# Room for a sixth raw weight pair, and the snapshots' pool opened behind the weight conversion

## The chip, the cores and the metric

The kernel runs on one core of one Trainium2 chip. The metric is the device time of one launch in microseconds (us), as the median of several runs. Before the change it is 868.43 us (three runs, 868.04 to 869.34).

The engines are named as in the profile: PE is the matrix engine and PEld its weight loads, DVE the vector engine, ACT the scalar engine, POOL the GpSimd engine, SP the engine that here issues nearly all DMAs. Each engine works through its own instructions in the order in which the program lists them; they meet at semaphores.

## The reference

Two blocks follow each other. An attention without softmax gives, by batch and head, a 64 x 64 matrix of keys by values, multiplies the queries with it and normalises each row; its output is reshaped to 4608 tokens of 512 features, and a feed-forward block with a squared ReLU follows.

```python
kv = np.einsum('bhsd,bhse->bhde', k, v)            # batch 8, heads 8, seq 576, dim 64
out = np.einsum('bhsd,bhde->bhse', q, kv)
rms = np.sqrt(np.mean(out * out, axis=-1, keepdims=True) + 1e-06)
x = (out / rms * g_norm)                           # -> (4608, 512)
h = x @ w_in                                       # (512, 2048)
r = np.maximum(h, 0.0)
return (r * r) @ w_out                             # (2048, 512)
```

The two weights arrive as 64-bit floats. The kernel reads them as 64-bit words and builds 32-bit floats from them.

## The kernel before

The 4608 tokens are cut into nine strips of 512. A strip is first multiplied "up" with `w_in`, then "down" with `w_out`; both products are made with Strassen-like schemes (seven products of half-size blocks in place of eight, in the later strips two levels deep), so sums and differences of weight blocks and of activations are needed beside the products. The order of the work is written out by hand: for each strip a list of steps, and between them the attention's slices for the next strips.

**Strip 0 is the opening, and the change lies in it.** Its 16 up steps (`up_first`, line 911, from 33.6 to 82.4 us in the profile) are plain products. Between them the weights are converted, one pair of pieces at a time (`convert`, with the table `PACE` that says how many conversions are done behind each step). One pair of pieces goes through these stages:

- SP asks for its two halves of 512 KB (`load_piece`, line 248) into a place of `raw_pool`; there are five places, each 8 KB per partition.
- ACT makes two passes over it (`act_words`, lines 260 and 262), into one of two `w_c` buffers and back into the raw place.
- POOL clamps (line 282), DVE puts the bits together in two passes (lines 284 and 288) into the 32-bit weight.
- For the last four of the sixteen pairs (`sums_out`) the result goes into a tile `wt`, which also has its room in `raw_pool`; DVE makes four sums there (line 306), and SP stores `wt` to DRAM as parts of `w_out`, four DMAs of 256 KB for each `wt` (line 336). Two further blocks go out at line 344.

`load_more` runs behind each conversion and asks for pieces up to `AHEAD` pieces beyond the converted ones: ten pieces are five pairs, as many as there are places. SP's queue is one list: the loads of keys, values and queries of the next batch (lines 135, 150, 165, 173), the raw pairs and the stores stand in it in the order in which the program issues them, and a DMA also waits for the semaphore that the eighth DMA before it used.

When the sixteen up steps are done, the rest is converted and the conversion's pools are closed (`conv.close()`, line 1402). In their room two pools open: `stream` (six tiles of 8 KB, weights streamed from DRAM) and `sum` (eight tiles of 2 KB). Both are opened with `reuse_waits="tile"`.

**The snapshots' pool** `c_pool` has six tiles of 2 KB per partition and is opened at line 92 with the long-lived pools, so it has room of its own. It holds copies of PSUM banks ("snapshots", `combine`, line 880), output tiles (`out_tile`, line 977) and, from strip 1 on, squares of attention outputs (line 493, through `query`). Its first tile is the snapshot of product 1 of strip 0's down pass.

**The work around that first snapshot**, in program order. Strip 0's down pass (`down`, line 870) runs its products in the order 1, 2, 5, 6, 7, 3, 4. ACT's list there reads: copy of transposed queries (line 422), the snapshot (line 880), two copies of the key-value matrices of batch 1's last pair of heads into `kv_all` (lines 453 and 454), squares of attention outputs (line 493). PE's list: product 1 (line 870), keys by values of that last pair (line 448), the attention outputs `x_ps` of two token tiles (line 484, pair of heads by pair of heads, the last pair last), product 2. The fourth pair of heads in line 484 needs the copies of lines 453 and 454. SP's list: the stores of the third and fourth `wt` (line 336), then the first streamed weights (line 965).

Of the kernel before, what the change touches and what calls it, by code (L numbers as in the profile page):

```python
# [20 lines left out]
def kernel(  # L21
# [56 lines left out]
    BEHIND = 1.6  # L78
    X_ON_PE = 2
    EPS = 1e-6  # L80
    AHEAD = 10
    PACE = (3, 4, 4, 5, 6, 7, 8, 9, 10, 11, 12, 13, 13, 14, 15, 16)
    const = ctx.enter_context(tc.tile_pool(name="const", bufs=1))
    wpool = ctx.enter_context(tc.tile_pool(name="wpool", bufs=1))
# [4 lines left out]
    small = ctx.enter_context(tc.tile_pool(name="small", bufs=3))  # L89
    g_pool = ctx.enter_context(tc.tile_pool(name="g", bufs=4))  # L90
    dram = ctx.enter_context(tc.tile_pool(name="dram", bufs=1, space=bass.MemoryType.DRAM))
    c_pool = ctx.enter_context(tc.tile_pool(name="c", bufs=6))
    conv = ExitStack()
    xt_pool = conv.enter_context(tc.tile_pool(name="xt", bufs=1))
    raw_pool = conv.enter_context(tc.tile_pool(name="raw", bufs=5))
    spare_pool = conv.enter_context(tc.tile_pool(name="spare", bufs=1))
    wtmp = conv.enter_context(tc.tile_pool(name="wtmp", bufs=2))
    psums = ExitStack()
# [62 lines left out]
    def load_rest(b, eng):  # L161
        h = b % 2 * (b > Q_ON_PE + 1)
        half = slice(REST * h, REST * (h + 1))
        for t, src in ((k_rest[half], k), (v_rest[half], v)):
            eng.dma_start(out=t, in_=src[b, :, C * P : S].rearrange("h s d -> s h d"))
# [20 lines left out]
    def load_next(q_eng=nc.sync, names="kvq"):  # L186
        u = next(to_load, None)
        if u is not None:
            load(*u, q_eng, names)
# [49 lines left out]
    raw = []  # L239
    raw_pairs = []  # L240

    def load_piece():
        i = len(raw)
        if i < len(sources):
            if i % 2 == 0:
                raw_pairs.append(raw_pool.tile([P, 2, 2, WN // 2], I64, name="raw", tag="raw"))
            t = raw_pairs[i // 2][:, i % 2]
            nc.sync.dma_start(out=t, in_=sources[i])
            raw.append(t)
# [50 lines left out]
    def load_more(end):  # L300

        while len(raw) < min(end + AHEAD, max(len(sources) - 4, end + AHEAD - 4), len(sources)):
            load_piece()
# [38 lines left out]
    def store_first(b):  # L342
        for e in range(2):
            nc.sync.dma_start(out=w_out[b, :, e], in_=w_first[b][:, :, ts(e, P)])
# [427 lines left out]
    def attend(n):  # L772
        while slice_at[0] < min(n, len(slices)):
            fn, a = slices[slice_at[0]]
            fn(*a)
            slice_at[0] += 1
# [582 lines left out]
    for s in range(N_STRIP):  # L1359
        attend(ready[s])  # L1360
        if s == DEEP_UP - 1:
            while queried:
                attend(slice_at[0] + 1)
            psums.close()
            fpsum = ctx.enter_context(tc.tile_pool(name="fpsum", bufs=5, space=bass.MemoryType.PSUM, reuse_waits="tile"))
            apsum = ctx.enter_context(tc.tile_pool(name="apsum", bufs=1, space=bass.MemoryType.PSUM, reuse_waits="tile"))
        if s >= DEEP_UP:
            steps = [(0.5, up_slot, (s, slot)) for slot in range(55)]
        elif s == 0:
            steps = [(2, up_first, (g, fh, i)) for g in range(NG) for fh in range(2) for i in range(2)]  # L1370
        else:
            steps = [(1, up, (s, g, p)) for g in range(NG) for p in ORDER]
        n_up = len(steps)
        if s < DEEP:

            steps += [(2, down, (s, p, i)) for p in (ORDER if s else (1, 2, 5, 6, 7, 3, 4)) for i in range(2)]
        else:
            steps += [(2, down_deep, (s, k, i)) for k in range(7) for i in range(2)]
        goal, begun = ready.get(s + 1, len(slices)), slice_at[0]
        if s >= DEEP_UP:  # L1380
            goal = max(goal, min(ready[DEEP_UP] + (len(slices) - ready[DEEP_UP]) * (s - 1) // (N_STRIP - DEEP_UP - 1), len(slices)))
            if s > DEEP_UP:
                goal = min(pair_ends, key=lambda end: abs(end - goal))
        total, done = sum(w for w, _, _ in steps), 0
        for i, (w, fn, a) in enumerate(steps):
            if s == 0 and i < n_up:

                if i == 0:
                    load_next()
                    load_rest(1, nc.sync)  # L1390
                    load_next()
                if i == 1:
                    load_next()
                if i == 2:
                    for b in range(2):
                        load_q_rest(b, nc.sync)
                if i == 14:
                    for b in range(2):
                        store_first(b)
            elif s == 0 and i == n_up:  # L1400
                convert(len(conversions))
                conv.close()

                stream_pool = ctx.enter_context(tc.tile_pool(name="stream", bufs=6, reuse_waits="tile"))
                sum_pool = ctx.enter_context(tc.tile_pool(name="sum", bufs=8, reuse_waits="tile"))
            if s == 0 and n_up <= i < n_up + 2:
                for g in range(2 * (i - n_up), 2 * (i - n_up) + 2):
                    sum_g1(0, g)
            if s == 0 and n_up + 2 <= i < n_up + 4:
                for g in range(2 * (i - n_up) - 4, 2 * (i - n_up) - 2):  # L1410
                    sum_g3(0, g)
            fn(*a)
            if s == 0 and i < n_up:

                convert(PACE[i])
            done += w
            if s:
                clock[0] += 3.2 if i >= n_up else 2.2 if s == DEEP else 1.2
                soon = tiles_due and tiles_due[0][2][0] // NT == s + 1
                if i == n_up + 10:  # L1420
                    while tiles_due and tiles_due[0][2][0] // NT == s + 1:
                        _, f, a = tiles_due.popleft()
                        f(*a)
                elif not due(keys_due) and not (soon and due(tiles_due)):
                    least = 2.1 if s == DEEP else 4.5 if i < n_up else 3.3
                    quiet = n_up * 2 // 3 < i < n_up + 3 or s == DEEP and (i > n_up + 9 or i == n_up + 7)
                    quiet = quiet or s == DEEP and i < n_up and drips and drips[0][0] == load_q_rest
                    if not quiet and clock[0] >= dripped[0] + least:
                        dripped[0] = clock[0]
                        drip(True)  # L1430
                        if s == DEEP and i == n_up + 8:
                            drip(True)
                if s == DEEP:
                    attend(begun + (goal - begun) * min(i + 1, 25) // 25)
                elif i < n_up:
                    attend_between(i, begun, goal, *(2, 34) if s == DEEP_UP else (0, 27), 38)
                if s == DEEP and i in (3, 4, 7, 9):
                    if i == 3:
                        last_sums = store_deep_sums(*deep_due.popleft())
                    next(last_sums, None)  # L1440
                if s == DEEP and i == n_up - 3:
                    leaf_sums(s, 4)
                if s == 1 and i in range(2, 23, 3):
                    deep_sums_in((1, 6, 5, 4, 0, 2, 3)[i // 3])
                if s == 1 and i in (17, 20, 21, 23):
                    stream()
                continue
            if i == n_up:
                nc.gpsimd.memset(open_xt(1)[:, 0, 0, 0:1], 0.0)
                stream(2)  # L1450
            if i == n_up + 4:
                stream()
            if i in (n_up + 8, n_up + 11):
                load(2, (i - n_up) // 11, nc.sync, "q")
            if i == n_up + 12:
                load_q_rest(2, nc.sync)
            if i - n_up in (7, 8, 9, 12):
                sums_in((7, 8, 9, 12).index(i - n_up))
            if i == n_up + 11:
                sums_x(1)  # L1460
            n = i + 1 - (n_up - 6)
            pairs, m = divmod(max(n - 2 * NP, 0), 3)
            attend(min(ready[0] + min(max(n, 0), 2 * NP) + (n >= 2 * NP) + 4 * pairs + (0, 2, 2)[m], goal))
            while deep_due and i not in (n_up + 1, n_up + 4, n_up + 12, n_up + 13):
                deque(store_deep_sums(*deep_due.popleft()), 0)
            if i == n_up + 2:
                store_first(2)
            if i == n_up + 3:
                for _ in range(2):
                    load_next(names="kv")  # L1470
            if i == n_up + 6:
                load_rest(2, nc.sync)
# [30 lines left out]
```

## Time and profile before

The profiled execution took 868.8 us, of which 867.0 us are the span from its first to its last instruction; 1.8 us lie around it.

| stretch, us | what runs | PE busy | DVE busy | ACT busy | DMA share |
|---|---|---|---|---|---|
| 0 to 20 | first attention slices | 15.4 of 20 | 5.5 | 9.0 | 0.92 |
| 20 to 65 | strip 0's up steps, conversion | 45.0 of 45 | 30.8 | 38.3 | 0.99 |
| 65 to 75 | the same | 9.71 of 10 | 8.0 | 9.9 | 0.75 |
| 75 to 100 | last conversions, down pass begins | 25.0 of 25 | 24.5 | 12.5 | 0.98 |
| 130 to 140 | last sums of strip 0 | 9.54 of 10 | 9.86 | 0.59 | 0.94 |
| 200 to 867 | strips 2 to 8 | 663.1 of 667 | 548.2 | 249.3 | 0.81 |

PE is busy in 99% of the span, DVE in 81%, ACT in 40%, POOL in 38%. The shares of DVE and ACT are much higher in the opening than in the mean. The granted TensorE clock is 1.00 throughout. "DMA share" is the mean busy share of the 16 DMA engines; values above 1 come from packets counted at the edges of a slice.

### The profile page before, as it was taken

How to read it: one execution, taken by the hardware profiler on the slowest of the kernel's cores; microseconds unless marked ns; L12 is line 12 of the kernel's file. 1: busy time of each engine (PE TensorE's matmuls, PEld its weight loads, DVE VectorE, ACT ScalarE, POOL GpSimd, SP SyncE). 2: the span in 40 equal slices, each digit the busy share in tenths (PEclk: the TensorE clock that was granted, in tenths of full speed). 3: DMA queues.
4: the chain of work that ended last, by engine and by line, in shares of the span. 5: the costliest groups of instructions: out<-in, count | busy, mean ns of one | idle time of the engine just before them, and what ended most of it. 6: DMA issues, size and time to landing. Idle time of an engine off the chain costs nothing.

```text
span 867.0 us, 32426 instructions
## 1 busy us (share of the span) xinstructions
PE 857.8 (99%) x14176; PEld 804.2 (93%) x14176; DVE 702.0 (81%) x1132; ACT 348.9 (40%) x777; POOL 328.1 (38%) x335
## 2 busy tenths in 40 slices
PE   7999999999999999999999999999999999999998
PEld 6445888889999999999999999999999999999998
DVE  3768988879877996789688967897889777975887
ACT  4888241320048303750356034901491148102810
POOL 1223004630458223730574045704470447145700
PEclk9999999999999999999999999999999999999999
DMA  9898998999999997989698979987678856885583
GB/s 307 277 362 269 274 377 239 295 332 353 280 264 259 342 325 233 228 307 344 209 244 273 341 239 281 283 297 270 198 236 302 301 165 221 293 282 196 175 315 121
DMA packets 169469, 236.46 MB, mean 273 GB/s; under 512 B 78704, under 2 KB 133744, under 8 KB 161008
## 3 DMA queue, kind: packets, MB, share of 16 engines
q1 hardware_dynamic: 169024, 234.33, 83.5%
q8 instruction: 111, 1.82, 0.9%
q14 instruction: 30, 0.25, 0.1%
q10 hardware_dynamic: 304, 0.07, 0.0%
HBM read 197.66 MB, written 36.70 MB: 270 GB/s over the span
## 4 chain that ended last, share of the span: by engine, by line
PE 83%; DMA 7%; DVE 5%; ACT 3%; SPq 1%; issue 1%; DVEq 0%; ACTq 0%
PE ps_A L865 36%; PE ps_B L865 31%; PE ps_C L865 5%; PE ps_A L870 4%; DMA raw<-in_moe_w_in_dram 2%; PE kv_ps L448 2%; PE x_ps L484 2%; PE ps_B L870 2%; DVE w_t L306 1%; DMA w_deep<-w_t 1%; DMA raw<-in_moe_w_out_dram 1%; DMA w_blk<-w_deep 1%; PE ps_C L870 1%; DMA first_qkv<-in_v_dram 1%; ACT w_c L260 1%
## 5 line engine op out<-in xcount | busy, mean ns | idle before, releaser
L865 PE MATMUL ps_B<-w_blk,g_s 128*64 128x128 f32 x2016 | 122.0, 273 | 0.0
L865 PEld LDWEIGHTS ps_B<-w_blk,g_s 128*64 128x64 f32 x2016 | 112.6, 137 | 0.1
L306 POOL TENSOR_TENSOR x_l<-xT 128x256 f32<-128x256 f32 x21 | 16.2, 773 | 230.2 <-PE ps_A L865 230.2
L865 PE MATMUL ps_B<-w_blk,gt 128*64 128x128 f32 x1504 | 94.1, 273 | 0.3 <-DMA w_blk<-w_deep 0.3
L865 PE MATMUL ps_A<-w_blk,g_s 128*64 128x128 f32 x1536 | 92.2, 273 | 0.0
L1323 POOL TENSOR_TENSOR snap<-snap,gt 128x512 f32<-128x512 f32 x35 | 46.2, 1320 | 112.5 <-ACT snap L1328 93.6
L865 PEld LDWEIGHTS ps_A<-w_blk,g_s 128*64 128x64 f32 x1536 | 85.7, 137 | 0.0
L865 PEld LDWEIGHTS ps_B<-w_blk,gt 128*64 128x64 f32 x1504 | 84.6, 137 | 0.8 <-PE ps_B L865 0.5
L1328 ACT COPY snap<-ps_A 128x512 f32<-128x512 f32 x63 | 36.8, 585 | 103.6 <-PE ps_A L865 96.2
L1263 ACT ACTIVATE gt<-gt 128x512 f32<-128x512 f32 x112 | 70.2, 627 | 9.9 <-DVE gt L1323 9.9
L1264 ACT ACTIVATE gt<-gt 128x512 f32<-128x512 f32 x112 | 70.7, 631 | 3.5
L865 PE MATMUL ps_A<-w_blk,gt 128*64 128x128 f32 x1152 | 71.2, 273 | 0.0
L865 PEld LDWEIGHTS ps_A<-w_blk,gt 128*64 128x64 f32 x1152 | 64.7, 137 | 0.0
L1112 ACT COPY o_sb<-ps_A 128x128 f32<-128x128 f32 x24 | 6.4, 265 | 144.7 <-PE ps_A L865 109.4
L306 DVE TENSOR_TENSOR gt<-gt 128x2048 f32<-128x2048 f32 (+1 forms) x29 | 59.7, 2063 | 0.0
L1111 DVE TENSOR_TENSOR o_sb<-o_sb,ps_B 128x256 f32<-128x256 f32 (+1 forms) x123 | 47.4, 386 | 14.3 <-ACT o_sb L1112 9.5
L865 PE MATMUL ps_A<-x_l,w_in 128*64 128x128 f32 x896 | 58.6, 273 | 0.2 <-DVE gt L1323 0.2
L1323 POOL TENSOR_TENSOR gt<-gt,snap 128x512 f32<-128x512 f32 x42 | 52.5, 1279 | 15.1 <-DVE snap L1323 15.1
L865 PEld LDWEIGHTS ps_A<-x_l,w_in 128*64 128x64 f32 x896 | 50.8, 137 | 0.5 <-DVE gt L1323 0.5
L865 PE MATMUL ps_B<-x_l,w_blk 128*64 128x128 f32 x784 | 51.2, 273 | 0.0
L865 PE MATMUL ps_A<-x_l,w_blk 128*64 128x128 f32 x784 | 51.2, 273 | 0.0
L1112 ACT COPY o_sb<-ps_B 128x128 f32<-128x128 f32 x31 | 8.2, 265 | 96.3 <-PE ps_B L865 96.3
(214 smaller groups left out, 1900.2 us busy)
## 6 DMA issues: line engine op xcount, KB each, us to landing
w_blk<-w_deep SPq DMA_DIRECT2D x56, 1024.0 KB, 7.3
w_blk<-w_out SPq DMA_DIRECT2D x56, 768.0 KB, 6.2
w_blk<-w_in_deep SPq DMA_DIRECT2D x49, 768.0 KB, 5.8
raw<-in_moe_w_in_dram SPq DMA_DIRECT2D x16, 512.0 KB, 9.2
raw<-in_moe_w_out_dram SPq DMA_DIRECT2D x16, 512.0 KB, 8.0
k<-in_k_dram SPq DMA_DIRECT2D x29, 256.0 KB, 4.9
v<-in_v_dram SPq DMA_DIRECT2D x29, 256.0 KB, 5.2
x_d<-x_q SPq DMA_DIRECT2D x27, 256.0 KB, 4.8
```

What stands on the lines that cost most here:

```text
L260: nc.scalar.activation(c, high_f, AF.Copy, scale=EXPONENT)
L306: eng.tensor_tensor(out=out, in0=a, in1=b, op=ALU.subtract)
L448: nc.tensor.matmul(ps[ts(h, D), i], lhsT=a, rhs=w, start=i == 0 and c == 0, stop=c == C, skip_group_check=True)
L484: nc.tensor.matmul(ps[half, r, i, ts(p, D)], lhsT=q[row, half], rhs=kvd[b, p][row, row], start=True, stop=True)
L865: nc.tensor.matmul(ps[half], lhsT=lhsT[:, half], rhs=rhs, start=start, stop=stop, skip_group_check=True)
L870: nc.tensor.matmul(bank[BANK[p]][:, i, :], lhsT=lhsT(k), rhs=rhs(k), start=p in (1, 5, 2) and i == 0 and k == 0, stop=k == n - 1, skip_gro ...
L1111: add = lambda out, a, b: nc.vector.tensor_tensor(out=out, in0=a, in1=b, op=ALU.add)
L1112: yield nc.scalar.copy(q[:, 3:4], small(1))
L1263: nc.scalar.activation(o, o, AF.Relu)
L1264: nc.scalar.activation(o, o, AF.Square)
L1323: add = lambda eng, out, a, b: eng.tensor_tensor(out=out, in0=a, in1=b, op=ALU.add)
L1328: nc.scalar.copy(t, ps)
```

## The change

`AHEAD` grows from 10 to 12 pieces and `raw_pool` from five to six places, so one more pair (8 KB per partition) is held, and pairs are asked for six ahead. `c_pool` is no longer opened at the start but behind `conv.close()`, in the freed room, ahead of `stream` and `sum`. It is opened without `reuse_waits="tile"`.

```diff
-    AHEAD = 10
+    AHEAD = 12
@@
     dram = ctx.enter_context(tc.tile_pool(name="dram", bufs=1, space=bass.MemoryType.DRAM))
-    c_pool = ctx.enter_context(tc.tile_pool(name="c", bufs=6))
     conv = ExitStack()
     xt_pool = conv.enter_context(tc.tile_pool(name="xt", bufs=1))
-    raw_pool = conv.enter_context(tc.tile_pool(name="raw", bufs=5))
+    raw_pool = conv.enter_context(tc.tile_pool(name="raw", bufs=6))
@@
                 conv.close()
 
+                c_pool = ctx.enter_context(tc.tile_pool(name="c", bufs=6))
                 stream_pool = ctx.enter_context(tc.tile_pool(name="stream", bufs=6, reuse_waits="tile"))
                 sum_pool = ctx.enter_context(tc.tile_pool(name="sum", bufs=8, reuse_waits="tile"))
```

In the built program the instructions of PE, DVE, ACT and POOL stand in the same order as before. In SP's list two raw loads move: pair 6 (of pairs 1 to 16) is asked for ahead of the keys, values and queries of batch 1, and each later pair takes the slot that the pair before it had. The conversion's room begins 12 KB lower than before. After `conv.close()` the six `c` tiles lie over the 8 KB of strip 0's transposed activations (`xT`) and over the first 4 KB of the raw place that the third `wt` used; `stream` and `sum` keep their addresses, and so lie half a raw place off the places they covered exactly before.

## The prediction

> **What bounds the kernel now.** The page's engine table comes first, then a table of busy time by stretch, in which the columns are the stretch, its length and the busy time of PE, PEld, DVE, ACT and POOL, then the clock, the DMA share and GB/s.
>
> ```profile
> PE 857.8 (99%) x14176; PEld 804.2 (93%) x14176; DVE 702.0 (81%) x1132; ACT 348.9 (40%) x777; POOL 328.1 (38%) x335
> ```
> ```profile
> 65.00:75.00 10.00, 9.71 (x62) 4.77 (x62) 8.00 (x8) 9.87 (x19) 3.96 (x3) 1.00 0.75 265
> 75.00:100.00 25.00, 25.00 (x197) 18.61 (x198) 24.45 (x36) 12.53 (x27) 2.84 (x3) 1.00 0.98 284
> 130.00:140.00 10.00, 9.54 (x45) 8.07 (x44) 9.86 (x16) 0.59 (x1) 0.00 (x0) 1.00 0.94 315
> ```
>
> PE sets the time: it stands still for 9 us of 867, and between 20 and 200 us almost only in the first and third of these stretches, 0.29 and 0.46 us. So a prefetch in the opening has under 1 us to win, while anything that stops PE is paid in full, since nothing later has slack to give it back.
>
> Next ACT's timeline (start, length, line, tiles; in brackets the idle time before, and what ended it), where the raw pairs are consumed:
>
> ```profile
> 45.14 1.17 ACT L260 ACTIVATE w_c<-raw 128x1024 f32<-128x1024 f32 x1 [0.50 <-DMA raw<-in_moe_w_in_dram]
> ...
> 53.38 1.14 ACT L260 ACTIVATE w_c<-raw 128x1024 f32<-128x1024 f32 x1 [1.60 <-DVE w_in L288]
> ...
> 57.53 1.16 ACT L260 ACTIVATE w_c<-raw 128x1024 f32<-128x1024 f32 x1 [0.78 <-DMA raw<-in_moe_w_out_dram]
> ```
>
> These are pairs 7, 9 and 10. The middle wait is named for DVE, but that pair's second half was issued at 45.85 and took 7.4 us to land, so it came at 53.3: also a raw wait. ACT loses 0.50 + 1.60 + 0.78 = 2.88 us to late raw pairs and then runs without a gap to 84 us.
>
> Last, the timeline where the first snapshot is taken:
>
> ```profile
> 88.75 8.14 SPq L336 DMA_DIRECT2D w_out<-wt  x8
> ...
> 90.71 0.59 ACT L880 COPY snap<-ps_A 128x512 f32<-128x512 f32 x1 [2.87 <-PE ps_A L870]
> ...
> 91.34 1.16 PE L484 MATMUL x_ps<-kv_all,qT 64*64 64x64 f32 x64
> ...
> 91.45 0.20 ACT L453 COPY kv_all<-kv_ps 64x64 f32<-64x64 f32 x1 [0.16 <-PE kv_ps L448]
> 91.68 0.21 ACT L454 COPY kv_all<-kv_ps 64x64 f32<-64x64 f32 x1
> ...
> 92.43 3.72 PE L870 MATMUL ps_C<-w_s,gt 128*128 128x256 f32 x16
> 92.56 1.09 ACT L493 ACTIVATE sq<-x_ps 128x512 f32<-128x512 f32 x2 [0.68 <-PE x_ps L484]
> ...
> 100.71 0.81 SPq L965 DMA_DIRECT2D w_blk<-w_out  x2
> ```
> ```profile
> SPq L965 <- DMA w_out<-wt: 3.6, 4, 1.4
> ```
>
> Today the snapshot waits for PE's product alone. The last `wt` stores are issued until 96.9 us, and SP's line 965 (second fence: waits in us, times, longest) waits for all of them, up to 100.6 us: that is when the last one lands.
>
> **The change, part by part.**
>
> *One more pair ahead.* Pairs 7 to 16 are asked for one SP slot earlier. Pair 6 is pushed in ahead of batch 1's loads, where 1 MB at the 406 GB/s of that stretch costs 2.6 us of transfer, but DMA then idles some 2.7 us between 28 and 35 us (shares 0.84, 0.75, 0.12, 0.63, 0.43 and 0.56 there). So the slots behind it slip by d, between 0 and 2.6 us; I take 1.5, the middle, because SP, with 0.5 us per issue, can't refill the idle piece wholly. Pair 10 then lands at 53.3 + d = 54.8 and is wanted at 57.53 - 2.88 = 54.65; pair 11 lands at 57.4 + d = 58.9 and is wanted, 2.88 earlier, at 57.9. Of the 2.88 us about 1.0 comes back as a wait. ACT and the conversion behind it run 1.8 us earlier (0.8 to 2.88). For PE this is worth the 0.29 us in the first stretch. It also brings the stores forward: the first `wt` waits for ACT's pass at 67.35, through POOL and DVE, whose chain of four `wt` tiles is without a gap from 70.09 to 92.66; the stores then fill the DMA queues from 78 to 98 us (share 1.01 to 1.17 in each 2 us slice to 98). All of it moves together, and the last landing goes from 100.6 to 98.8 us (97.7 to 99.8; 100.6 if ACT wins nothing).
>
> *The snapshots' pool in the freed room.* In the built program the first snapshot (line 880) now waits, beside PE, for the semaphores of all eight last `wt` stores and for DVE's last sum: those of the fourth `wt` too, whose place the pool does not touch. ACT, done with the queries' copy at 87.85, stands at that snapshot until 98.8 instead of 90.7 us. Queued behind it: both copies to `kv_all`, then the squares. PE gets through three quarters of line 484, to 91.34 + 0.75 x 1.09 = 92.16 us, and needs the last pair's copies for the rest. They end 1.05 us after the snapshot begins (0.59 + 0.20 + 0.21 and starts; 1.18 before, with a wait of 0.16 in it), at 99.85. PE stands for 99.85 - 92.16 = 7.7 us; product 2 is next in its list and cannot pass. The 0.29 us saved above is swallowed.
>
> What follows is late by the same amount or less. DVE finds the squares at about 100.9 in place of 94.99 us, 5.9 later, so it gains nearly 2 us on PE; that removes the 0.46 us at 130 to 140 us, where PE waits for DVE. SP issues on, with streamed weights 9 us nearer than before.
>
> *PE's speed after the gap.* No row before shows PE after an idle time over 1.41 us, save the start:
>
> ```profile
> 1.36 3.22 PE L392 MATMUL t_ps<-ident 128*128 128x128 f32 x14 [1.36 <-POOL ident masks.py:199]
> ```
> ```profile
> 103.33 1.04 PE L654 MATMUL xt_ps<-ident,x_n 128*128 128x128 f32 x8
> 104.20 3.62 PE L870 MATMUL ps_B<-w_s,g_s 128*128 128x256 f32 x16
> ```
>
> The first fourteen start (4.51 - 1.36) / 14 = 225 ns apart, those of the same shape in mid-kernel (104.20 - 103.33) / 8 = 109 ns: the slow start loses 14 x 0.116 = 1.6 us. After a gap of 7.7 us the loss lies between 0 (as after 1.41 us) and about twice that start, 3.2 us. I take 1.6, because 7.7 us is a case nearer to the start. The Trainium skill ("TensorE: Matmul & The Clock Gate", Part 1) says that an idle window of about 3.4 us halves PE's clock until such a window has been busy; an estimate by it is 1.7 to 3.4 us lost, up to 1.8 above my term. The clock column shows 1.00 even at the slow start, so it can neither bear this out nor refute it.
>
> *New waits at no cost.* POOL's write into strip 1's `xT` (82.57) now waits for the third `wt`'s stores, landing near 97; behind it POOL has nothing until 142 us, and the reader, ACT's copy at 103.97, is itself some 8 us later. Without that cover it would hold ACT as the snapshot does. DVE's first output sum (108.44) waits for the same stores, 10 us after they land; SP's line 965 adds waits on work that ended by 85 us.
>
> *Sum*, against the profiled execution (867.0 us span + 1.8 us around it = 868.8, 0.4 above the median): +7.7 - 0.46 + 1.6 = +8.9 us. On the median of 868.43 this is 877.3 us.
>
> **The rivals.**
>
> A. *PE keeps its speed through the gap.* Then +7.2, 875.6 us. For it: no slow matmuls in mid-kernel so far. Against it: no gap of this length either.
>
> B. *The last stores do not come forward*, because the pushed-in pair delays the rest by all of d = 2.6 us and more, or DMA sets the pace by itself: landing at 100.6, PE free at 101.65, a stop of 9.5 us, with a slow restart of 1.6 to 3.2 us and nothing back from DVE: 879.5 to 881.1 us. For it: DMA is full from 35 to 65 us. Against it: pairs 8 to 11 have 3 to 4 us more each.
>
> C. *The stores land early enough* (the other side). The wait decides only from the point where the last store lands after 91 us. If DVE's chain moved up 2.88 us it would end at 89.8, and an isolated `wt` store takes 2.3 us from issue (at 76 us); were the queues empty, the last of four, issued 0.55 us apart, would land near 94 and PE stop 3 us. Only if the eight semaphores are met before the snapshot is reached do the gains stand alone: -0.29 - 0.46, 867.7 us. Against it: 4.0 MB of `wt`, 2.0 MB of line 344 and 0.8 MB of loads must pass between the first `wt` and there, and did so in 24.6 us.
>
> D. *The prefetch does nothing* and the room costs nothing is the same as C without the gains, 868.4 us.
>
> **How the numbers follow.** My forecast (a stop near 7.7 us and a slow restart) gets 0.53 and 877.3 us, its own range 876.2 to 878.3 for d from 0 to 2.6; A 0.25; B 0.12; C and D together 0.04; the remaining 0.06 is a stop of only 3 to 5 us, 871.5 to 874. The range 874.0 to 880.0 holds the forecast, A (from 874.6, with d = 0) and the lower part of B. What a measurement of this kernel tells from no change is about 0.2%, 1.7 us: slower 0.95, same 0.03, faster 0.02.
>
> **What would show it.** Right: ACT's raw waits of 0.50, 1.60 and 0.78 us gone or under 1.2 us in all; ACT idle for 10 to 11 us before the first snapshot, released by a `w_out<-wt` DMA at 98 to 100 us; PE idle 7 to 9 us inside line 484, released by ACT line 454; the matmuls of the next 3 us longer than 379 ns, their usual length; no idle PE at DVE's sum near 145 us; all else shifted. Wrong: the snapshot released by PE alone, ACT's gap before another instruction, PE's idle time of 9 us in the span unchanged, or a stop that later stretches give back.

## The result, and the profile after

| | median, us | runs | lowest to highest | ratio to before, 95% interval |
|---|---|---|---|---|
| before, beside it | 869.24 | 6 | 868.04 to 871.50 | |
| changed | 879.45 | 6 | 877.58 to 886.53 | 1.0125, 1.0088 to 1.0162 |

The change makes the kernel slower by 1.25%, 10.2 us. The profiled execution of the changed kernel took 880.8 us, its span 879.0. The diff takes out a line near the top, so from there to line 1402 each line has a number one lower: the snapshot is now L879, the attention outputs L483, the `wt` stores L335, the streamed weights L964.

The engine table of the page: PE's share falls from 99 to 98% while its number of instructions stays.

```profile
PE 860.9 (98%) x14176; PEld 806.9 (92%) x14176; DVE 701.8 (80%) x1132; ACT 348.6 (40%) x777; POOL 328.5 (37%) x335
```

The busy times of the three stretches shown before (stretch, length, busy time of PE, PEld, DVE, ACT, POOL; clock, DMA share, GB/s):

```profile
65.00:75.00 10.00, 10.00 (x45) 4.82 (x45) 8.93 (x9) 9.79 (x19) 2.58 (x3) 1.00 0.59 215
75.00:100.00 25.00, 16.88 (x158) 12.06 (x157) 16.48 (x21) 8.26 (x19) 2.62 (x3) 0.88 0.96 277
130.00:140.00 10.00, 10.00 (x48) 8.83 (x47) 9.79 (x16) 4.44 (x3) 0.00 (x0) 1.00 0.65 194
```

The two short waits of before, 0.29 and 0.46 us, are gone (nor are they in the list of PE's waits over the whole span); in the middle stretch PE lost 8.12 us, and for the first time the mean clock is below 1. The timeline of the changed kernel shows where:

```profile
89.49 0.93 PE L483 MATMUL x_ps<-kv_all,qT 64*64 64x64 f32 x48
94.98 0.10 POOL L1449 MEMSET xT<- 128x1 f32 x1 [14.41 <-DMA w_out<-wt]
...
97.78 0.81 SPq L964 DMA_DIRECT2D w_blk<-w_out  x2
97.80 0.58 ACT L879 COPY snap<-ps_A 128x512 f32<-128x512 f32 x1 [11.80 <-DMA w_out<-wt]
98.28 0.21 ACT L452 COPY kv_all<-kv_ps 64x64 f32<-64x64 f32 x1
...
98.54 0.93 PE L483 MATMUL x_ps<-kv_all,qT 64*64 64x64 f32 x16 [8.12 <-ACT kv_all L452]
99.40 6.00 PE L869 MATMUL ps_C<-w_s,gt 128*128 128x256 f32 x16
```

Read it from below. Product 2 takes 6.00 us in place of 3.72. Ahead of it PE stood for 8.12 us, after 48 of the 64 products of line 483, for ACT's copy to `kv_all`. ACT had stood 11.80 us before its snapshot, and what let it go was a store of `wt` landing: SP's line 964, which waits for all those stores, goes out in the same instant (97.78).

The raw pairs in ACT's timeline, against 0.50, 1.60 and 0.78 us before:

```profile
53.70 1.16 ACT L259 ACTIVATE w_c<-raw 128x1024 f32<-128x1024 f32 x1 [0.87 <-DMA raw<-in_moe_w_out_dram]
57.68 1.16 ACT L259 ACTIVATE w_c<-raw 128x1024 f32<-128x1024 f32 x1 [0.58 <-DMA raw<-in_moe_w_out_dram]
```

The clock around the stop, in stretches of 2 us, columns as above:

```profile
92.00:94.00 2.00, 0.00 (x0) 0.00 (x0) 0.00 (x0) 0.00 (x0) 0.00 (x0) 0.95 1.15 346
94.00:96.00 2.00, 0.00 (x0) 0.00 (x0) 0.00 (x0) 0.00 (x0) 0.10 (x1) 0.50 1.11 333
...
102.00:104.00 2.00, 2.00 (x6) 1.55 (x6) 1.79 (x7) 0.00 (x0) 0.00 (x0) 0.50 1.04 438
104.00:106.00 2.00, 2.00 (x13) 1.77 (x12) 1.97 (x4) 0.12 (x1) 0.00 (x0) 0.99 0.16 66
```

The granted clock halves some 3.4 us after PE stops and comes back only at 104, 5.5 us after PE works again.

Last, PE's two longest waits by sum, from the view of waits (us, times, longest):

```profile
PE x_ps L483 <- ACT kv_all L452: 8.1, 1, 8.1
PE x_ps L483 <- issue: 3.1, 2, 2.8
```

Nearly all of the second, 2.8 us, lies at 270 us, in a later strip, and "issue" means that this view shows nothing that PE waited for; what it was is read below, under e8 and e9. The trace of before has none of it.

**How the lag grows.** The start of the same DVE reciprocals (the square root's part of each normalisation) in each profiled execution, less that of before, in us; minus is earlier. The e-numbers are the experiments below; e9 is the changed kernel itself, profiled a second time.

| before, us | changed | e9, the same | e1 | e2 | e4 | e5 | e10, as e5 | e8 |
|---|---|---|---|---|---|---|---|---|
| 21.93 | -1.34 | -1.63 | -0.33 | -0.63 | -1.72 | -1.42 | -1.41 | +0.93 |
| 111.44 | +9.26 | +8.99 | -0.84 | +12.41 | +5.67 | +6.89 | +6.87 | +9.22 |
| 185.09 | +8.26 | +7.99 | -0.97 | +11.42 | +4.67 | +5.89 | +5.88 | +8.22 |
| 250.81 | +8.90 | +8.00 | -0.95 | +13.71 | +6.08 | +5.90 | +6.71 | +8.23 |
| 264.99 | +11.93 | +8.04 | -0.94 | +14.23 | +6.05 | +8.92 | +8.87 | +8.22 |
| 353.70 | +11.92 | +9.00 | -1.30 | +14.20 | +6.19 | +10.28 | +9.68 | +11.08 |
| 606.26 | +12.00 | +8.52 | -0.04 | +14.33 | +11.90 | +10.49 | +12.99 | +12.84 |

Up to 111 us the lag is what the opening does, but the first row shows that executions differ by over 1 us at 22 us already: most are ahead of the trace of before there, and so is e6 (1.79 us), which has neither the sixth pair nor the stop. What is added later differs from kernel to kernel, and between two executions of one kernel (first two columns, from 111 us to the last row: +2.74 and -0.47). The kernel before varies too: it took 866.7 to 877.9 us over all its runs here.

### The profile page after: what moved, and what is told of

Read it like the earlier page. It is cut to its first block, busy times and chain, and to the rows that moved or that the text cites. A ratio compares the mean times of both kernels' runs of the same rounds, so it can differ in the third digit from the quotient of the medians.

```text
span 879.0 us, 32431 instructions
## 1 busy us (share of the span) xinstructions
PE 860.9 (98%) x14176; PEld 806.9 (92%) x14176; DVE 701.8 (80%) x1132; ACT 348.6 (40%) x777; POOL 328.5 (37%) x335
## 4 chain that ended last, share of the span: by engine, by line
PE 85%; DMA 6%; ACT 4%; DVE 2%; issue 1%; SPq 1%; POOL 0%; DVEq 0%; ACTq 0%
PE ps_A L864 35%; PE ps_B L864 30%; PE ps_A L869 6%; PE ps_C L864 5%; PE ps_B L869 3%; PE x_ps L483 2%; DMA raw<-in_moe_w_in_dram 2%; PE ps_C L869 2%; PE kv_ps L447 2%; DMA w_blk<-w_in_deep 1%; DMA raw<-in_moe_w_out_dram 1%; ACT w_c L259 1%; DMA k_rest<-in_k_dram 1%; ACT raw L261 1%; DVE wt L305 1%
```

## The experiments

The theory: the snapshots' pool, opened in the conversion's room without `reuse_waits="tile"`, makes ACT's first snapshot wait for every last `wt` store; PE stops behind it, and starts again at half clock. The rival for the stop is the sixth pair, whose loads might hold something up; the rivals for its size are a clock that plays no part, and a landing set by something other than the stores' own queue.

### e1: the same room, but waits tile by tile

```diff
-                c_pool = ctx.enter_context(tc.tile_pool(name="c", bufs=6))
+                c_pool = ctx.enter_context(tc.tile_pool(name="c", bufs=6, reuse_waits="tile"))
```

> One word of the change differs: the snapshots' pool is opened in the freed room with waits by tile, as the two pools behind it are. My theory (the first snapshot waits for the last wt stores, because its pool's waits are taken for the whole freed room): its first tile lies over xT, which PE has long read, so the snapshot waits for PE alone, PE has no idle time inside line 483 and no slow clock, and the time is that of the kernel before less what the earlier raw pairs win, 0 to 0.8 us: ratio to before 0.998 to 1.001. Rival 1 (the sixth pair's transfers, not the wait, cost the time): still 8 to 12 us slower, ratio 1.009 to 1.014. Rival 2 (the room itself hurts later, by the order in which the six tiles are taken): 1.003 to 1.014 with idle time spread over the strips.

Measured: 869.79 us (12 runs) against 869.25, ratio 0.9998 (0.9981 to 1.0014). The timeline of e1 at the same place:

```profile
89.87 0.59 ACT L879 COPY snap<-ps_A 128x512 f32<-128x512 f32 x1 [2.87 <-PE ps_A L869]
...
90.50 1.16 PE L483 MATMUL x_ps<-kv_all,qT 64*64 64x64 f32 x64
...
91.59 3.72 PE L869 MATMUL ps_C<-w_s,gt 128*128 128x256 f32 x16
```

PE's product releases the snapshot as before, line 483 runs through its 64 products, product 2 has its 3.72 us. The sixth pair and the shared room are both still there, so the loss is the pool's whole-room wait alone. And what the prefetch brings by itself can't be told from nothing in these runs. The granted clock says the same: its mean over the span is 0.998 to 1.000 in the twelve runs of e1, and 0.988 to 0.996 in all 14 runs of the changed kernel (six above, eight as e9).

### e2: the room alone, without the sixth pair

```diff
-    AHEAD = 12
+    AHEAD = 10
-    raw_pool = conv.enter_context(tc.tile_pool(name="raw", bufs=6))
+    raw_pool = conv.enter_context(tc.tile_pool(name="raw", bufs=5))
```

> Only the room part of the change: snapshots' pool opened in the freed room as in the change, but five raw places and ten pieces ahead. My theory: the snapshot waits for the last wt store as in the change, and that store now lands where it did before (10 us behind the snapshot of the kernel before, not 7 to 8), so PE stops 9 to 10 us and then runs some 5.5 us at half clock: 11 to 13 us slower than before, ratio 1.0125 to 1.015. Rival (the sixth pair is to blame): ratio 0.999 to 1.001.

Measured: 881.78 us (4 runs), ratio 1.0152 (1.0115 to 1.0188). In its timeline:

```profile
100.88 0.58 ACT L879 COPY snap<-ps_A 128x512 f32<-128x512 f32 x1 [12.86 <-DMA w_out<-wt]
...
101.62 0.93 PE L483 MATMUL x_ps<-kv_all,qT 64*64 64x64 f32 x16 [9.18 <-ACT kv_all L452]
```

Half of the change does all of the damage: the stores land at 100.88 in place of 97.80. Between these two executions the sixth pair brings the landing 3.1 us forward and thereby softens the other half.

### e6: that room with tile waits, five places

e2 with e1's edit: before's prefetch, the pool behind the conversion.

> Room part of the change alone with waits by tile for the snapshots' pool: five raw places, ten pieces ahead. Against the run with waits by tile and the sixth pair it shows what the sixth pair is worth. My theory: ACT's raw waits are back at 2.9 to 3.5 us (1.3 to 1.5 us with the sixth pair), PE stands 0.3 to 1.1 us near the queries' transposes at 70 us, and the time is within 0.2% of the kernel before, at most 1 us above the one with the sixth pair: ratio 0.999 to 1.002. Rival (the sixth pair is worth more, hidden by something else): 1.002 or more.

Measured: 869.93 us (12 runs) against 870.43, ratio 0.9998 (0.9979 to 1.0017). e1 and e6 differ by the sixth pair, and both ratios are 0.9998. In the opening e6 had one wait more, `t_ps` for ACT's `qT`, 1.6 us; it doesn't show in the time.

### e4: other stores out of the way

The stores of line 343 for the weight blocks 0 and 1 are moved from step 14 to behind the first streamed weights.

```diff
-                if i == 14:
-                    for b in range(2):
-                        store_first(b)
...
             if i == n_up + 2:
-                store_first(2)
+                for b in range(3):
+                    store_first(b)
```

> The changed kernel, with the four 512 KB stores of the weight blocks w_s (line 343) moved in SP's list from ahead of the third wt to behind the first streamed weights. My theory (the stop ends when the last wt store lands): 2 MB less stand before that store, it is issued when DVE has finished the fourth wt (near 89 us) and lands at 92 to 95 us, so ACT's snapshot starts 3 to 5 us earlier than in the changed kernel, PE stops 3 to 5.5 us, and the time is 3 to 5 us below the changed kernel (more if the stop is too short for the half clock): ratio to before 1.004 to 1.009. Rival (the stop is set by something else than that landing): stop of 8 us as before, ratio 1.0115 to 1.014.

Measured: 874.31 us (6 runs), ratio 1.0070 (1.0042 to 1.0097). Its timeline:

```profile
94.10 0.81 SPq L964 DMA_DIRECT2D w_blk<-w_out  x2
94.15 0.58 ACT L879 COPY snap<-ps_A 128x512 f32<-128x512 f32 x1 [8.53 <-DMA w_out<-wt]
...
94.89 0.93 PE L483 MATMUL x_ps<-kv_all,qT 64*64 64x64 f32 x16 [4.85 <-ACT kv_all L452]
...
95.75 6.06 PE L869 MATMUL ps_C<-w_s,gt 128*128 128x256 f32 x16
```

With 2 MB fewer in the queues the last `wt` lands 3.7 us earlier and the stop is 3.3 us shorter: the stop ends with that landing. The restart costs the same after 4.85 us as after 8.12 (6.06 against 6.00 us). The execution profiled here took 880.8 us, the other five 873.1 to 875.2: it has two later waits for a weight from DRAM, 4.0 us in all, 3.2 of them at 387 us with 3.4 us at half clock behind, and its lag grows by 4.95 us there, between 354 and 424 us.

### e7: the pools in another order

```diff
-                c_pool = ctx.enter_context(tc.tile_pool(name="c", bufs=6))
                 stream_pool = ctx.enter_context(tc.tile_pool(name="stream", bufs=6, reuse_waits="tile"))
                 sum_pool = ctx.enter_context(tc.tile_pool(name="sum", bufs=8, reuse_waits="tile"))
+                c_pool = ctx.enter_context(tc.tile_pool(name="c", bufs=6))
```

> The changed kernel with the snapshots' pool opened behind the stream and sum pools and not ahead of them, still without waits by tile. It then lies over the converted-word buffers w_c and no raw place, and its first snapshot waits for DVE's last reading of w_c (near 87 us) in place of the stores. My theory (what counts is which freed tiles the pool lies over): that reading is over before PE's product 1 is, so the snapshot waits for PE alone, there is no stop and no half clock: ratio to before 0.998 to 1.001. Rival (any pool opened without waits by tile in the freed room waits for all of it): a stop of 8 us and ratio 1.0115 to 1.014.

Measured: 873.20 us (12 runs), ratio 1.0034 (1.0017 to 1.0050): a miss. The snapshot is free (at 88.53, released by PE), but the timeline has the old wait on another engine:

```profile
88.83 0.68 DVE L305 TENSOR_TENSOR wt<-w_s,wt 128x512 f32<-128x512 f32 x1
98.21 2.50 DVE L896 TENSOR_TENSOR g_s<-gt 128x512 f32<-128x512 f32 x4 [8.70 <-DMA w_out<-wt]
```

The first sums of strip 0's down pass now lie where `wt` was, and wait for its stores, tile waits or not. That costs less because PE has product 2 and more to do meanwhile; it then waits 2.3 + 1.6 + 1.1 us for DVE. In both orders an engine waits for the stores; what it costs depends on who needs that engine's next work.

### e3, e5 and e10: PE kept busy through the stop

Fillers, products with the identity into the part of `x_ps` that is written next anyway, ahead of the last pair of heads in the first line 483; 26 in e3, 38 in e5 and e10.

```diff
+            if p == NP - 1 and not warmed:
+                warmed.append(1)
+                for _ in range(WARM):
+                    nc.tensor.matmul(ps[:, 0, 0, ts(p, D)], lhsT=ident, rhs=ident[:, 0:D], start=True, stop=True)
```

> The changed kernel, with 26 further matmuls (identity by identity, 64 columns, written to a part of x_ps that the next real product overwrites) put into PE's list at the place where PE stops in line 483. They need nothing from ACT and so fill some 5 to 7 of the 8 us of the stop. My theory (2.3 to 2.8 us of the loss are PE's half clock after the stop): the stop ends when it did, the granted clock stays at 1.00, the sixteen matmuls of product 2 take 3.7 us and not 6.0, and the time is 2 to 3 us below the changed kernel: ratio to before 1.008 to 1.010. Rival (the slow matmuls come from the weights' or DMA traffic, not from the idle time): product 2 keeps 6.0 us, ratio 1.0115 to 1.014.

Measured: 880.63 us (4 runs), ratio 1.0130 (1.0102 to 1.0158). A miss of the experiment: the fillers took 6.02 us and ended 3.4 us too early, and in that time the clock fell again, to 0.50 from 99.1 to 105.9.

> As the run with 26 further matmuls, which ended 3.4 us before the stop did and left the half clock in place; now 38, at the 0.23 us that one took there 8.8 us, the whole stop. My theory (the half clock comes from PE standing still, and costs 2.3 to 2.8 us): the clock stays at 1.00 through product 2, whose sixteen matmuls take 3.7 us and not 6.0 to 6.5, and the time is 2 to 3 us below the changed kernel: ratio to before 1.0075 to 1.010. Rival (something else that the stop brings slows product 2): 6.0 us or more for product 2, ratio 1.0115 to 1.014.

Measured: 880.85 us (4 runs), ratio 1.0119 (1.0092 to 1.0146). Its timeline (lines five higher here):

```profile
99.31 3.72 PE L874 MATMUL ps_C<-w_s,gt 128*128 128x256 f32 x16
```

No idle time at the stop, no half clock, product 2 at its usual 3.72 us. At 111 us its lag is 6.89, 2.37 us less than the changed kernel's, although the fillers hold the last sixteen products of line 488 until 98.92, 0.38 us later than there: the price of the half clock is the sum, 2.75 us, shown where it arises. The time, though, did not fall.

> e5 again, on the same chip as the changed kernel itself (e9). Theory: without the half clock the lag at 110 us is 2.4 us less, and the time is 1.5 to 2.5 us below that of e9. Rival: the 2.4 us are given back whole, and the two times agree within their intervals.

Measured: 881.47 us (6 runs) against 879.11 for e9 on the same chip (ratios to before 1.0111, 1.0069 to 1.0153, and 1.0085, 1.0056 to 1.0114). The lag at 111 us is again 2.4 us less than in the changed kernel's first profile (6.87), 2.1 less than in e9, and ends at 12.99. The rival holds for the total, though why is not shown: in the executions profiled, the lag grows after 185 us by 4.6 us in e5 and 7.1 in e10, more than the fillers win at 100 us.

### e8 and e9: is a delay paid twice?

e8 has e5's fillers and e1's tile waits: a delay of 8.7 us of pure work. e9 is the changed kernel unaltered.

> The 38 filler products of e5 are put ahead of the last pair of the first line 488, but the snapshots' pool waits tile by tile as in e1: no stop and no half clock are left, only 8.7 us of extra TensorE work at the place where the changed kernel stops. Theory (a delay at this place costs its own length and nothing more): 869.8 + 8.7 = 878.5 us, and the lag on the kernel before stays what it is at 110 us. Rival (any delay there is paid a second time later, where loads then collide and TensorE waits for issue near 265 us): lag at 110 us near 8, at the end 10 to 11, 880.5 to 881.5 us, as e5 showed.

> The changed kernel as it is, beside e8 and e10 on one chip. If the idle time for issue near 270 us belongs to this schedule, it comes again, 2 to 3 us long and within a few us of the same place; if it is chance, it is gone or elsewhere, and the lag at the end is near that at 110 us. Time 879 to 881 us either way.

Measured: e8 881.30 us (6 runs), ratio 1.0108 (1.0068 to 1.0149); e9 879.11 us (8 runs), ratio 1.0085 (1.0056 to 1.0114). e8's lag at 111 us is 9.22, 8.3 more than the 0.93 it had at 22 us; 4.6 more come after 185 us, without any stop or half clock behind them. e9 has the stop (8.6 us) and the slow product (5.56 us) and then keeps its lag. So a delay is not always paid twice, and the 2.8 us at 270 us are no fixed part of the change: one execution of it has them, another hasn't.

Of what the later loss consists, PE's timelines tell in part. First e8:

```profile
296.60 1.09 PE L869 MATMUL ps_B<-w_blk,gt 128*64 128x128 f32 x16 [1.76 <-DMA w_blk<-w_deep]
359.21 0.34 PE L488 MATMUL x_ps<-kv_all,qT 64*64 64x64 f32 x5 [1.48 <-issue]
451.65 0.34 PE L488 MATMUL x_ps<-kv_all,qT 64*64 64x64 f32 x7 [0.34 <-issue]
548.62 0.45 PE L488 MATMUL x_ps<-kv_all,qT 64*64 64x64 f32 x12 [0.95 <-issue]
```

Then e10:

```profile
271.67 0.66 PE L869 MATMUL ps_A<-x_l,w_blk 128*64 128x128 f32 x8 [2.36 <-issue]
...
548.77 0.45 PE L488 MATMUL x_ps<-kv_all,qT 64*64 64x64 f32 x12 [2.27 <-issue]
```

Two kernels with the same PE list stand at the same place (with twelve products of line 488 left, near 548.7 us), for 0.95 and 2.27 us; e5 and e10 both stand in the middle of the same `ps_A`, 2.10 and 2.36 us. The same places come back; whether PE stands there, and how long, varies.

The traces show what PE lacks there: its own instructions. DMA brings them in blocks of 16 KB, and the page of the changed kernel counts the blocks (packets, MB, share of the 16 DMA engines):

```profile
q8 instruction: 111, 1.82, 0.8%
```

PE's 28352 matmuls and weight loads make 255 to a block. There are 23 waits for issue on PE in the twelve traces, none of them in before and e9. Every one ends at the same place in a block (193 to 195 of these instructions past a multiple of 256), and 1.2 to 1.8 us after the transfer of a block has ended; mostly a block has landed some 4 us before PE comes to that place. So PE stands where its next block came late. Why it came late, and why it takes over 1 us more to be used, no run shows. The fillers add 152 instructions to the list and so move every later block; whether what e5, e8 and e10 lose after 185 us is the fillers' own doing is not tested either.

## Why the prediction was right or wrong

**The mechanism was right.** ACT's snapshot waits for the `wt` stores (e1 takes that wait away and the whole loss goes), the `kv_all` copies are queued behind it, and PE stops three quarters through line 484 (483 in the changed kernel). Nearly all of it is paid: of the 9.26 us of lag at 111 us, 1.0 has come back by 185 us. POOL's write to `xT` waited for the stores as foreseen, 14.41 us, at no cost, and PE's wait for DVE's sum is gone. Three signs were missed by a little: the raw waits are 1.45 us and not under 1.2, ACT's gap is 11.80 us and not 10 to 11, and the landing at 97.8 us lies just ahead of 98 to 100.

**The step that failed is PE's restart.** The sum has it at 1.6 us, the loss of the kernel's first fourteen products; it was 2.75 us, 2.3 in e9. And "all else shifted" put at nothing what the later strips add, which was 3.74 us in one execution and 0.53 in another.

**The forecast was 2.15 us too low** (877.3 against 879.45), inside the range of 874.0 to 880.0. Of this 0.81 us lie in the kernel before, 869.24 beside the changed one and 868.43 when the forecast was made. The change was to add 8.9 us; it added 10.2, and on e9's chip 8.0 (879.11 against 871.16). The forecast ratio, 877.3 / 868.43 = 1.0102, lies within the intervals of both. So the total can't tell which term was off; the terms can:

- *Raw waits.* About 1.0 us was to come back; 0.87 + 0.58 = 1.45 did. ACT won 1.43 us, not 1.9.
- *The landing.* "The last landing goes from 100.6 to 98.8 us": it came at 97.8. In the other traces with the sixth pair and the stores in the same order, SP's line that waits for it goes out between 96.96 (e5) and 99.21 us (e8), and with five places between 100.32 (e6) and 100.87 (e2). The gain of 1.8 us is inside that spread and below its middle, about 2.5. In the changed kernel it did not come out of ACT's 1.43 us alone; from where the rest came was not tried.
- *The stop.* 7.7 us was forecast and 8.12 measured (8.59 in e9), but as a lag the stop weighed less: PE took up the last quarter of line 483 at 98.54, 6.4 us behind the 92.16 reckoned for before, where 7.7 was forecast. It had arrived 1.7 us earlier, 1.3 of which it already had at 22 us, where the trace of before is a late one (e6 is 1.79 us ahead of it too). A stop that ends with a landing swallows whatever PE won ahead of it. Against e1, whose last quarter begins at 90.50 + 0.75 x 1.09 = 91.3 us, the stop weighed 7.2 us, and 7.4 in e9, close to the forecast.
- *The restart.* "I take 1.6": this term is the one that was mis-sized. The 16 products of line 483 took 0.93 us (0.46 in e8, at full clock) and product 2 6.00 instead of 3.72: 0.47 + 2.28 = 2.75 us; in e9 0.47 + 1.84 = 2.3; by e5 2.75 again; in e2 and e4 2.8 and in e3 3.2. The row taken for it was the start of the kernel, where the loss ends with fourteen products; here PE runs 5.5 us at half clock (4.6 in e9). The upper bound, twice the start's loss, 3.2 us, held it. The Trainium skill ("TensorE: Matmul & The Clock Gate", Part 1) puts half clock after an idle window of about 3.4 us, until such a window has been busy, from which the estimate was 1.7 to 3.4 us; the trace agrees, 2.3 to 2.75.
- *The clock column.* "It can neither bear this out nor refute it" was wrong: it shows 0.50 for 10.2 us here. What made the kernel's own start slow at a column of 1.00 stays open.
- *Together.* 7.7 + 1.6 = 9.3 us of lag behind the opening were forecast, 9.26 and 8.99 measured: 6.4 + 2.75 = 9.15. This was luck: the restart was taken too small, and the trace of before, against which the lag is counted, began late. Against e1, which is 0.84 us ahead of it at 111 us, the lag is 10.1 and 9.8 us.
- *What comes back.* 0.46 us at DVE's sum was to go; that stretch is full now, and the lag falls by 1.0 by 185 us in both executions.
- *"All else shifted".* From 185 us to 606 us the lag grows by 3.74 in the profiled execution and by 0.53 in e9's. The latter took 877.32 us, the forecast itself, and is the fastest of its eight; their median is 879.11. That the others pick up such losses is likely and not shown, since only these two were profiled. Nor does it take a stop: e1 picks up 0.93 there, e6 2.5, e8 4.6. The waits named are those for issue, which is late instructions, and for weights from DRAM; whether a shifted list meets more of them is not settled.

**The rivals.** A, PE keeps its speed, falls with the clock of 0.50 and the 6.00 us. B, the stores not brought forward, is what e2 shows when the sixth pair is left out: landing at 100.88, a stop of 9.18, 881.78 us; B had said 9.5 and up to 881.1. C, stores early enough, did not happen; e4 goes part of its way, with a stop of 4.85 us, and comes out at 874.31, just past the 871.5 to 874 that had been set on a stop of 3 to 5 us. D fell with the first profile.

No version here beats the kernel before: e1 and e6 are level with it.

## What to carry to other kernels

A pool opened in the room of closed pools inherits their last users: ask of its first tile which DMAs read the old one, when they land, and what stands behind the waiting instruction on its engine; let it wait tile by tile, and give that place first to work that nobody needs soon. A stop that ends with a DMA's landing eats what the engine won ahead of it, and behind PE's stops of 3.4 to 9.2 us here the half clock cost a further 2.3 to 3.2 us. When PE is busy 99% of the time, a prefetch that removes waits of ACT has only PE's own few tenths to win.

## What the hardware showed that was not expected

- The half clock lasts 10.2 us in the changed kernel (93.8 to 104.0), in e9 and in e2, 6.8 us in e3 and e4: three and two times 3.4 us. What falls behind the stop differs less, 5.5 us after one of 8.12 and 5.6 after one of 4.85 (e4), so the shorter stop cost as much afterwards.
- In e5 a wait of 2.10 us near 270 us was followed by 3.4 us at half clock, while the 2.8 us in the changed kernel and the 2.36 us of e10 had none; 3.2 us in e4, at 387 us, were followed by 3.4 us of it again. For these short waits the length of the idle time alone doesn't decide. The windows of e5, columns as above:

```profile
270.00:271.00 1.00, 0.41 (x6) 0.41 (x8) 0.30 (x2) 0.00 (x0) 0.92 (x3) 0.90 0.32 93
271.00:272.00 1.00, 1.00 (x14) 1.00 (x12) 0.00 (x0) 0.41 (x1) 1.00 (x1) 0.50 0.99 257
```

- PE's waits for issue, 0.2 to 2.8 us, all at the border between two 16 KB blocks of its instruction list; 13 of the 23 lie in line 483 (488 with fillers).
